# Two attention blocks on one core: the first block's output tiles move into a written-out cycle of one whole unit of the second block

## The chip, the core and the metric

The kernel runs on one core of a Trainium2 chip. The metric is device time in microseconds (us) of one execution; the number compared is the median of several executions. Five engines take part: TensorE (PE, with its weight loads shown apart as PEld), VectorE (DVE), ScalarE (ACT), GpSimd (POOL), and SyncE (SP), which issues the DMAs. Each runs its own instructions strictly in the order in which the program lists them for it, and waits on semaphores for the others.

## The reference

Both inputs are 2048 tokens wide 512, with 32 heads of 16. Block A is attention with a sliding window of 256 keys, block B is full attention. The result is the two outputs side by side.

```
qkv = (x @ wqkv) -> q, k, v per head           # both blocks
s   = (q @ k^T) * 16 ** -0.5                   # A: only keys j with 0 <= i - j < 256
p   = softmax(s)
out = concat_heads(p @ v) @ wo                 # 2048 x 512, for A and for B
```

## The kernel before

**Tiling.** A unit is one group of four heads (g, 8 of them) times one chunk of 512 queries (c, 4 of them), so that each block has 32 units. Block A is done first, and its order doesn't change here. In the stage of block B a unit has 16 steps, one for each 128 keys. A step is four scores and one weighing.

**What PE does in that stage.** There are four kinds of work, and the strings below name them by letters:

- `s`: one score, one matmul of 51 rows by 512 queries (`scores`, line 713). ACT then takes the exponential out of PSUM (line 720).
- `m`: half of one maximum, one matmul of 48 rows by 512 keys (`max2`, line 557), for a unit that comes one or two units later. DVE reduces it out of PSUM (line 560). Two `m` make a pair; `M` is a pair whose two banks one DVE instruction reduces together. A unit has 64 scores and 64 halves of maxima.
- a digit: that many quarters of a weighing (`weigh2`, line 745), p times v, for 128 queries each. A `4` is a whole weighing: eight instructions in four column tiles of the array, into the one bank 0.
- `g`: one step of two output tiles of block A (`half_step`, line 440), a matmul of 64 rows for each of the two tiles. Two tiles of 128 tokens make a pair of output tiles and take 24 `g`, 12 and then 12 with the row halves exchanged between the two banks. Block A has 16 such tiles, so 8 pairs. ACT copies the two finished banks out (`put_out`, line 868), and SP stores them.

`s`, `m` and `g` use half of the array's rows each, and two that follow each other in different halves run side by side. In the text such an instruction is called a half matmul, and two side by side a slot. A weighing uses the array in another arrangement, so that going from half matmuls to a weighing and back costs time.

**Order.** It is written out by hand: the main loop walks strings of letters, the cycles, and issues what each letter says. Cycles are chosen one after the other:

```
MANY = "ssm4mssMs2msms2sM"
FEW = "msmms4msssmsm4ss"
OUTS = "mgggmmggmsgggmsgmmgmggmm44smgsmmgggsgsmggmssggmggg"
...
        if np_ == total:
            cycle = LAST
        elif two and two[-1][0] <= ns / HG * STEP and max(operands(x[3]) for x in two) <= M.t["PE"]:
            cycle = OUTS
        ...
        else:
            cycle = FEW if lead >= LEADM + 1 / 32 else MANY
```

`ns` counts scores, `np_` pairs of maxima, and `two` are the next two output tiles of block A, taken when they are due and their inputs (`x_o`, the normalised and split heads) are there. Each of `MANY`, `FEW` and `OUTS` has 8 scores, that is 2 of a unit's 16 steps. `MANY` has 4 pairs of maxima, `FEW` has 3, and `OUTS` has 8 with all 24 `g` of a pair of output tiles. An `OUTS` runs ahead with the maxima (`lead`), and `FEW` then gives that lead back. Before the last stage there are 14 MANY, then 8 OUTS and 32 FEW in mixed order, then 192 MANY; then come 11 LAST, which have no maxima.

**Banks.** PSUM has eight banks: 0 for the weighing, and seven that the loop's model of the engines (`Loop`) deals out, to whichever of the allowed ones is free first. `ROOMS` gives the allowed ones for scores and for maxima: in FEW four and three, in MANY three, two for single halves and a fixed two for `M`; in OUTS five in common, since banks 6 and 7 take the two output tiles.

**What hangs on a unit's maxima.** When the last pair of a unit is done, POOL puts together the maxima of four key chunks and splits them into parts (`max_chunk` and `max_finish`, lines 631 to 656). PE then transposes the parts (`max_rows`, line 677), ACT copies them (line 679), and two DMAs write them into rows of the unit's queries. The unit's first score needs these rows. Beside this, POOL normalises finished heads (`normalise_now`, lines 840 to 843).

Of the kernel before, what the change touches and what calls it, by code (L numbers as in the profile page):

```python
# [20 lines left out]
HG = 4  # L21
# [16 lines left out]
STEP = 2.45  # L38
# [2 lines left out]

MANY = "ssm4mssMs2msms2sM"
FEW = "msmms4msssmsm4ss"
OUTS = "mgggmmggmsgggmsgmmgmggmm44smgsmmgggsgsmggmssggmggg"
LAST = "4ssssfssss4"
PACES = {FEW: 2.25, MANY: 2.45, OUTS: 5.4, LAST: 2.45}
ROOMS = {FEW: (range(4), range(4, 7)), MANY: (range(3), range(5, 7)), OUTS: (range(5), range(5)),
         LAST: (range(5), range(5))}
LEADM = 1.25
QU = 2.4  # L50


# [103 lines left out]
class Loop:  # L156
# [51 lines left out]
        self.free[n] = self.act + 100  # L208
        return n

    def halves(self, ready):
        for a in range(2):
            end = self.matmul(a, ready)
        return end

# [19 lines left out]
def attention_kernel(ctx: ExitStack, tc: tile.TileContext, xT, wqk, wv, wo, out):  # L235
# [9 lines left out]
    M = Model()  # L245
    ready = {}
    obank = [None]
    ns = 0
# [65 lines left out]
    ps_all = psum.tile([128, 8, QC], F32, name="ps_all")  # L314
# [114 lines left out]
            half_step(q, pairs, [view(bank) for bank in banks])  # L429
        M.pe("h", CHUNK * 233)  # L430

    def half_step(q, pairs, ps):

        turn, q = divmod(q, 12)
        k, i = divmod(q, 3)
        u, v = ((0, 0), (0, 1), (1, 0))[i]
        for a in range(2):
            l, r = pairs[a ^ turn][k]
            rows = slice(64 * a, 64 * a + 64)
            op = nc.tensor.matmul(ps[a ^ turn], l(u)[rows], r(v)[rows], start=turn == q == 0,  # L440
                                  stop=turn == 1 and q == 11)
            if turn and q == a == 0:
                tc.add_manual_dep(op.ins, min(since)[2].ins.name, LANDED, reason="the row tiles change banks")

    def heads_of(b, g, s, a):
# [222 lines left out]
    def max_rows(b, g, c):  # L668
        n = f"{b}_{g}_{c}"
        nm = parts["nm"].bitcast(BF16).rearrange("p a s (n u) -> p a (s n) u", u=2)[:, :, :, 1]  # L670
        if slot[0]:
            bank, ps = None, ps_all[:, 1 + loop.rows()]
        else:
            bank, ps = room()
        ps = ps.bitcast(BF16)
        for a in range(2):
            nc.tensor.transpose(ps[32 * a:32 * a + 32, :128], nm[:, a], ident)  # L677
        nt = sb.tile([64, 128], F32, name=f"ntr_{n}", tag="ntr")
        op = nc.scalar.activation(nt, ps[:64, :128], AF.Copy)
        t = mark(op, M.run("ACT", 200, M.pe("c", 80)))  # L680
        release(bank, t)
        for a in range(2):
            ready["q", b, g, c] = M.dma(12, t)
            nc.sync.dma_start(opq[b, g, c][ROW[a] + KS:ROW[a] + KM].bitcast(F32).rearrange(
                "s r (q t) -> s (r q) t", t=128), nt[32 * a + 8:32 * a + 32])
# [180 lines left out]
    def put_out(b, c, qt, ps):  # L866
        ob = row(f"ob_{b}_{c}_{qt}")
        nc.scalar.activation(ob, ps, AF.Copy)  # L868
        t = M.run("ACT", 480, M.t["PE"] + WAKE)
        nc.sync.dma_start(out[c * QC + 128 * qt:c * QC + 128 * qt + 128, b * D:(b + 1) * D], ob)  # L870
        M.dma(256, t)
        return t

    def pairs_out(b, c, qt):
        return [(lambda u, p=p: osp[b, p, c][:, u, 128 * qt:128 * qt + 128], lambda v, p=p: ws[b, "o", p][:, v])
                for p in range(NG // 2)]
# [89 lines left out]
    def operands(it, n=0):  # L966

        f, b, *a = it
        if f == project_qk:
            keys = [("w", b, a[0], a[1])] + [("x", b, a[2], i) for i in range(4)]  # L970
            t = (slots_st + [M.NEVER] * 2)[n] - 2700 + LAND_V
        elif f == project_v:
            keys = [("w", b, "v", i) for i in range(4)] + [("x", b, a[0], i) for i in range(4)]
            t = (slots_v + [M.NEVER] * 2)[n] - 2700 + LAND_V
        else:
            keys = [("w", b, "o", i) for i in range(4)] + [("o", b, i, a[0]) for i in range(4 if len(a[1]) == 1 else 3)]
            t = 0
        return max(t, *(ready.get(k, M.NEVER) for k in keys))
# [137 lines left out]
    stage, two, banks, turned = 0, None, None, None  # L1116
    todo_a = list(ORDER_A)
    while todo_a or gen[0]:
# [7 lines left out]
        x = "p" if gen[0] else todo_a[0]  # L1126
# [5 lines left out]
        t = NEVER  # L1132
        if gen[0]:
            t = pe
# [118 lines left out]
    loop = Loop()  # L1253
# [9 lines left out]
    while nq < 4 * len(steps):  # L1263
        two = heapq.nsmallest(2, proj)
        lead = np_ / 32 - ns / 64
        if np_ == total:
            cycle = LAST
        elif two and two[-1][0] <= ns / HG * STEP and max(operands(x[3]) for x in two) <= M.t["PE"]:
            cycle = OUTS
            two = [heapq.heappop(proj)[3][1:] for _ in two]  # L1270
            two = [(b, c, qts[0]) for b, c, qts in two]
            nh, ready_h, end_h = 0, max(loop.free[5:]) + loop.SEM, 0
            now[0] = ns / HG * STEP
        else:
            cycle = FEW if lead >= LEADM + 1 / 32 else MANY
        loop.rooms = ROOMS[cycle]
        for x in cycle:
            k = ns // HG
            if x == "s" and k < len(steps):
                if ns % HG == 0:  # L1280
                    t = k * STEP
                    t0 += int(1000 * PACES[cycle])
                    M.t["PE"] = max(M.t["PE"], t0)
                    settle()
                    while todo and todo[0][0] <= t:
                        pop()
                scores(1, *steps[k], ns % HG)
                side = ns % 2
                ns += 1
            elif x in "Mm" and np_ < total:  # L1290
                if not filled:
                    filled = True
                    for _ in range(FILL):
                        nc.tensor.matmul(ps_all[:, 0, 0:256], mone[:, 0], mone, start=True, stop=True)
                if x == "M":
                    sides = (0, 1)
                elif other is None:
                    sides = (0,) if cycle == MANY else (1 - side,)
                    other = 1 - sides[0]
                else:  # L1300
                    sides, other = (other,), None
                u, n = divmod(np_, 32)
                kc, n = divmod(n, 8)
                g, c = units[NA + u][1:]
                n1 = loop.maximum(sides)
                max2(g, c, kc, *divmod(n, 2), sides, ps_all[:, 1 + n1:1 + n1 + len(sides)])
                side = sides[-1]
                if other is None:
                    np_ += 1
                    if np_ % 8 == 0 and np_ % 32 > 8:  # L1310
                        max_chunk(g, c, np_ % 32 // 8 - 1)
                    if np_ % 32 == 0:
                        max_finish(1, g, c)
                        rows.append((k + 1, (1, g, c)))
            elif x == "g":
                if nh == 12:
                    ready_h = max(ready_h, loop.first + loop.SEM)
                half_step(nh, [pairs_out(*y) for y in two], [ps_all[:, 6], ps_all[:, 7]])
                end_h = loop.halves(ready_h)
                nh += 1  # L1320
                if nh == 12:
                    since.clear()
                    loop.first = M.NEVER
                if nh == 24:
                    for n1, y in enumerate(two):
                        put_out(*y, ps_all[:, 6 + n1])
                        loop.copies(5 + n1, end_h)
            elif x == "f" and k < len(steps) and not rows:

                for _ in range(6):  # L1330
                    if gen[0] or proj and proj[0][0] <= k * STEP and operands(proj[0][3]) <= M.t["PE"]:
                        advance()
                        loop.outs(0, 1)
                        half_tile += 1
                        if half_tile % 12 == 0:
                            advance()
                t0 += 650
            elif x.isdigit():
                if 0 <= nq < 4 * len(steps):
                    g, c, kt = steps[nq // 4]  # L1340
                    q = nq % 4
                    weigh2(g, c, kt, 128 * q, 128 * (q + int(x)))
                    loop.weigh(int(x))
                    if kt == NT - 1 and q + int(x) == 4:
                        unit_end(1, g, c)
                nq += int(x)

                if rows and rows[0][0] <= k and nq % 8 == 0:
                    max_rows(*rows.pop(0)[1])
    assert not rows  # L1350
    normalise(1, NG // 2 - 1, NQC - 1)
    while todo or proj or gen[0] or soon:
# [28 lines left out]
```

## Time and profile before

| | us |
|---|---|
| median of 3 runs | 1805.34 (1803.41 to 1806.23) |
| profiled execution | 1804.34 |
| its span, first to last instruction | 1802.6 |

The granted TensorE clock was 0.997 over the span. Stages of block B in the profiled execution, by the start of the first exponential of each:

| stage | from, us | to, us | scores |
|---|---|---|---|
| 14 MANY | 519.0 | 587.5 | 112 |
| 8 OUTS and 32 FEW | 587.5 | 821.1 | 320 |
| 192 MANY | 821.1 | 1716.6 | 1536 |
| 11 LAST | 1716.6 | 1764.7 (last exponential) | 80 |

A row of the timeline gives start, duration, engine, line, operation, what it writes and reads, the number of instructions merged into it, and in brackets the engine's idle time before it with what ended it. A matmul shown with x8 is eight instructions. Durations of single matmuls are longer than the distance between them, since they overlap: starts are what counts.

### The profile page before, as it was taken

The page shows a single profiled execution, that of the slowest core. Times are in us where ns is not written, and L with a number is a line of the kernel's source. Part 1 is how long each engine was busy: PE and PEld are TensorE (multiplying, and loading weights), DVE is VectorE, ACT ScalarE, POOL GpSimd, SP SyncE. Part 2 cuts the span into 40 slices and gives each one's busy share as a digit, 9 for nine tenths or more (in the row PEclk, how much of TensorE's full clock was granted, in tenths as well). Part 3 has the DMA queues.
Part 4 walks back from the last instruction along what each step waited for, and adds up shares of the span by engine and source line. Part 5 has one row for each costly group of instructions (what it writes and reads, how often), then busy time and mean ns, then how long its engine had stood idle before and what let it go on. Part 6 is the DMA issues. An engine that isn't in the chain of part 4 may idle for free.

```text
span 1802.6 us, 39006 instructions
## 1 busy us (share of the span) xinstructions
PE 1779.8 (99%) x14926; PEld 913.2 (51%) x14926; DVE 1524.2 (85%) x2324; ACT 1403.5 (78%) x2749; POOL 648.6 (36%) x1334
## 2 busy tenths in 40 slices
PE   8999999999999999999999999999999999999998
PEld 6776657767754555433444444444444444444436
DVE  4766786677789888889999999999999999999901
ACT  4466676655569676799999998999999999999983
POOL 0377888655745331034311024231012322022320
PEclk9999999999999999999999999999999999999999
DMA  8776667545562122311200311130031121010112
GB/s 266 200 215 192 192 205 226 172 144 173 188 195 81 66 98 61 77 29 48 60 23 31 66 39 29 31 77 16 16 77 35 29 64 37 17 54 8 32 37 94
DMA packets 129355, 166.80 MB, mean 93 GB/s; under 512 B 23204, under 2 KB 59044, under 8 KB 129156
## 3 DMA queue, kind: packets, MB, share of 16 engines
q1 hardware_dynamic: 129168, 164.31, 31.3%
q8 instruction: 117, 1.92, 0.5%
q14 instruction: 70, 0.57, 0.1%
HBM read 94.49 MB, written 68.19 MB: 90 GB/s over the span
## 4 chain that ended last, share of the span: by engine, by line
PE 90%; DVE 5%; ACT 2%; DMA 2%; SPq 1%; issue 1%; POOL 0%; ACTq 0%; DVEq 0%; POOLq 0%
PE ps_all L745 28%; PE ps_all L557 19%; PE ps_all L713 18%; PE ps_all L440 10%; PE ps_all L305 8%; PE ps_all L760 4%; DVE mt L560 4%; PE ps_all L603 3%; ACT p L720 1%; DMA in<-xT_A 1%; DVE nm L613 1%; SPq L469 0%; PE ps_all L677 0%; DVE ps_all L612 0%; ACT ob L868 0%
## 5 line engine op out<-in xcount | busy, mean ns | idle before, releaser
L720 ACT ACTIVATE p<-ps_all 128x512 f32<-128x512 f32 x2432 | 1263.5, 598 | 214.1 <-PE ps_all L713 129.2
L560 DVE TENSOR_REDUCE mt<-ps_all 128x1 f32<-128x512 f32 (+1 forms) x1596 | 1209.5, 832 | 52.8 <-PE ps_all L557 42.6
L713 PE MATMUL ps_all<-oq,opk 51*128 51x512 f32 (+2 forms) x2752 | 757.6, 406 | 4.0 <-ACT p L720 1.5
L557 PE MATMUL ps_all<-opk,oq 48*128 48x512 f32 x2016 | 672.5, 436 | 2.0 <-ACT ob L868 0.9
L745 PE MATMUL ps_all<-p,vt 128*17 128x256 f32 (+1 forms) x5736 | 576.7, 476 | 1.8 <-ACT ou L771 1.7
L713 PEld LDWEIGHTS ps_all<-oq,opk 51*128 51x128 f32 x2752 | 389.1, 186 | 194.9 <-ACT p L720 156.1
L557 PEld LDWEIGHTS ps_all<-opk,oq 48*128 48x128 f32 x2016 | 311.9, 185 | 305.8 <-DVE mt L560 187.1
L731 POOL TENSOR_SCALAR_AFFINE_SELECT p<-p 128x256 f32<-128x256 f32 x480 | 179.0, 407 | 113.0 <-ACT p L720 111.8
L745 PEld LDWEIGHTS ps_all<-p,vt 128*17 128x17 f32 x5736 | 97.2, 95 | 223.5 <-issue 210.8
L612 DVE COPY_PREDICATED ps_all<-mone,ps_all 128x256 f32<-128x256 uint16 x224 | 95.4, 426 | 84.7 <-PE ps_all L603 78.6
L613 DVE TENSOR_REDUCE nm<-ps_all 128x2 f32<-128x512 f32 x224 | 155.3, 693 | 7.7
L629 POOL TENSOR_TENSOR mu<-mt 128x16 f32<-128x16 f32 x31 | 6.9, 222 | 405.2 <-DVE mt L560 405.2
L631 POOL TENSOR_TENSOR mu<-mt,mm 128x16 f32<-128x16 f32 x62 | 13.7, 220 | 385.4 <-DVE mt L560 385.4
L440 PE MATMUL ps_all<-x,w 64*128 64x512 f32 x720 | 119.2, 393 | 0.0
L305 PE MATMUL ps_all<-x,w 128*128 128x512 f32 x408 | 102.7, 400 | 2.0 <-ACT x L253 1.3
L760 PE MATMUL ps_all<-p,vt 128*17 128x384 f32 (+2 forms) x1408 | 95.4, 391 | 0.0
L603 PE MATMUL ps_all<-opk,oq 48*128 48x384 f32 (+2 forms) x512 | 92.3, 364 | 2.4 <-ACT vst L504 0.8
L799 POOL TENSOR_TENSOR rd<-ld,minus 128x32 f32<-128x32 f32 x15 | 81.9, 5458 | 20.2 <-DMA ld<-od 20.2
L440 PEld LDWEIGHTS ps_all<-x,w 64*128 64x128 f32 x720 | 84.5, 185 | 8.8
L305 PEld LDWEIGHTS ps_all<-x,w 128*128 128x128 f32 x408 | 74.2, 188 | 24.3 <-ACT p L720 2.7
L388 ACT ACTIVATE raw<-ps_all 128x512 f32<-128x512 f32 x56 | 32.3, 596 | 67.9 <-PE ps_all L305 53.1
L440 PE MATMUL ps_all<-w_v,x 64*128 64x512 f32 x432 | 81.1, 391 | 0.0
(79 smaller groups left out, 1039.6 us busy)
## 6 DMA issues: line engine op xcount, KB each, us to landing
parts<-st SPq DMA_DIRECT2D x64, 512.0 KB
oq<-parts SPq DMA_DIRECT2D x128, 128.0 KB
opk<-parts SPq DMA_DIRECT2D x128, 128.0 KB
od<-ou SPq DMA_DIRECT2D x64, 256.0 KB
vd<-vst SPq DMA_DIRECT2D x32, 272.0 KB
oq<-parts SPq DMA_DIRECT2D x128, 64.0 KB
opk<-parts SPq DMA_DIRECT2D x128, 64.0 KB
t<-od SPq DMA_DIRECT2D x32, 256.0 KB
```

Of the source, the lines that this page charges most:

```text
L305: nc.tensor.matmul(ps, l(u), r(v), start=start and k == 0, stop=stop and k == n - 1)
L440: op = nc.tensor.matmul(ps[a ^ turn], l(u)[rows], r(v)[rows], start=turn == q == 0, stop=turn == 1 and q == 11)
L557: nc.tensor.matmul(ps[:, a - lo], q[rows, 128 * qt:128 * qt + 128], k[rows, kc * QC:kc * QC + QC], start=True, stop=True)
L560: op = nc.vector.tensor_reduce(out=m[:, kc, lo:lo + len(sides), r, qt], in_=ps, axis=AX.X, op=ALU.max)
L603: nc.tensor.matmul(two[:, a, 0:w], opq[b, g, c][rows, r, 128 * qt:128 * qt + 128], opk2(g)[rows, r, t0:t1], start=True, stop=True)
L612: nc.vector.copy_predicated(two[:, :, 256:384], later, two[:, :, 0:128])
L613: op = nc.vector.tensor_reduce(out=m[:, :, r, qt, 0], in_=two[:, :, 128:384], axis=AX.X, op=ALU.max)
L713: nc.tensor.matmul(ps[x][:, col:col + n1], opk2(g)[rows, pr, 128 * k:128 * k + 128], opq[b, g, c][rows, pr, q0:q0 + n1], start=True, stop= ...
L720: op = nc.scalar.activation(p[:, a0 + x, :w], ps[x][:, :w], AF.Exp, scale=SCALE)
L731: nc.gpsimd.affine_select(out=v, in_=v, pattern=[[0, 2], [sign, 128]], compare_op=ALU.is_ge, fill=zero_fill, base=base, channel_multiplier ...
L745: nc.tensor.matmul(o[32 * j:32 * j + VW, q0:q1], vt[(g // 2) % 2][:, kt, vc:vc + VW], pts[1, g, c, kt, j // 2][:, j % 2, q0:q1], start=kt ...
L760: nc.tensor.matmul(o[32 * j:32 * j + VW, q0:q0 + w], vt[(g // 2) % 2][:, kt, vc:vc + VW], pts[b, g, c, m, j // 2][:, j % 2, col:col + w], ...
```

## The change

OUTS becomes a cycle of a whole unit: 64 scores, 32 pairs of maxima, all as single halves `m`, 16 weighings and the 24 `g` of one pair of output tiles. It begins only where the scores stand at 56 of a unit's 64 (`PHASE`), so that it runs from eight scores before one unit's end to eight before the next one's. Four new letters change the allowed banks on the way: `[` allows all seven for scores and maxima in common, `(` five in common (banks 6 and 7 go to the output tiles from here on), `)` issues the two copies of the finished tiles and allows seven again, and `]` goes back to four and three. The letter `t` gives the place of the transposes inside the cycle; in the other cycles they stand where they did. A `g` now starts with the row half that the instruction before it did not use.

With that there are 15 MANY, 8 OUTS of a unit each, one after the other, then 167 MANY, and the same 11 LAST; FEW is not used any more. The work in the stage is the same: the 8 units hold the 512 scores and 256 pairs of maxima that 24 MANY, 32 FEW and 8 OUTS held.

```
-OUTS = "mgggmmggmsgggmsgmmgmggmm44smgsmmgggsgsmggmssggmggg"
+OUTS = "[smssmm4ssmsmms4smsssmm4mmssmms4smmmss4smmmss4msmmss(4smmgsgsgmgsmsggmsggmsgmsmggmgmmm44msgmsggsmsgmsggmsgmgsmgsmggmsgmm)4mssmss4smsmsm4smsmms4msssmm4smmsmss4smsmtssmmmss4s]"
-PACES = {FEW: 2.25, MANY: 2.45, OUTS: 5.4, LAST: 2.45}
+PACES = {FEW: 2.25, MANY: 2.45, OUTS: 2.6, LAST: 2.45}
-ROOMS = {FEW: (range(4), range(4, 7)), MANY: (range(3), range(5, 7)), OUTS: (range(5), range(5)),
-         LAST: (range(5), range(5))}
+ROOMS = {FEW: (range(4), range(4, 7)), MANY: (range(3), range(5, 7)), OUTS: (range(4), range(4, 7)),
+         LAST: (range(5), range(5)), "[": (range(7), range(7)), "(": (range(5), range(5)),
+         ")": (range(7), range(7)), "]": (range(4), range(4, 7))}
+PHASE = 56
...
-    def half_step(q, pairs, ps):
+    def half_step(q, pairs, ps, first=0):
-        for a in range(2):
+        for a in (first, 1 - first):
...
-            if turn and q == a == 0:
+            if turn and q == 0 and a == first:
                 tc.add_manual_dep(op.ins, min(since)[2].ins.name, LANDED, reason="the row tiles change banks")
...
-        elif two and two[-1][0] <= ns / HG * STEP and max(operands(x[3]) for x in two) <= M.t["PE"]:
+        elif two and ns % 64 == PHASE and two[-1][0] <= ns / HG * STEP and max(operands(x[3]) for x in two) <= M.t["PE"]:
             cycle = OUTS
-            nh, ready_h, end_h = 0, max(loop.free[5:]) + loop.SEM, 0
...
+            elif x in "[()]":
+                loop.rooms = ROOMS[x]
+                if x == "(":
+                    nh, ready_h, end_h = 0, max(loop.free[5:]) + loop.SEM, 0
+                if x == ")":
+                    for n1, y in enumerate(two):
+                        put_out(*y, ps_all[:, 6 + n1])
+                        loop.copies(5 + n1, end_h)
             elif x == "g":
-                half_step(nh, [pairs_out(*y) for y in two], [ps_all[:, 6], ps_all[:, 7]])
-                end_h = loop.halves(ready_h)
+                half_step(nh, [pairs_out(*y) for y in two], [ps_all[:, 6], ps_all[:, 7]], 1 - side)
+                end_h = loop.halves(ready_h, 1 - side)
...
-                if nh == 24:
-                    for n1, y in enumerate(two):
-                        put_out(*y, ps_all[:, 6 + n1])
-                        loop.copies(5 + n1, end_h)
...
-                if rows and rows[0][0] <= k and nq % 8 == 0:
+                if rows and rows[0][0] <= k and nq % 8 == 0 and cycle != OUTS:
                     max_rows(*rows.pop(0)[1])
+            elif x == "t" and rows:
+                max_rows(*rows.pop(0)[1])
```

Three places show it. The line numbers after the change are two higher (557 becomes 559, 713 becomes 715, 745 becomes 747, 440 becomes 442). In the rows `opk` and `oq` are keys and queries, with the operand named first telling scores (`oq` first) from maxima (`opk` first); `w_o` and `x_o` are the weights and inputs of an output tile, `p` and `vt` those of a weighing.

PE, the last steps of a pair of output tiles of block A's second 512 tokens before the change, up to the weighing behind them:

```order
L440 MATMUL ps_all<-w_o_6686,x_o_2_1_7790 128x512 x4
L557 MATMUL ps_all<-opk_76,oq_1_0_7869 128x512
L440 MATMUL ps_all<-w_o_6777,x_o_3_1_7993 128x512 x6
L557 MATMUL ps_all<-opk_76,oq_1_0_7869 128x512
L713 MATMUL ps_all<-oq_0_2_6760,opk_75 128x512
L557 MATMUL ps_all<-opk_76,oq_1_0_7869 128x512 x2
L713 MATMUL ps_all<-oq_0_2_6760,opk_75 128x512
L745 MATMUL ps_all<-p_0_2_8_0_8319,vt_77 17x512 x2
L745 MATMUL ps_all<-p_0_2_8_1_8370,vt_77 17x512 x2
```

The same on PE after the change:

```order
L442 MATMUL ps_all<-w_o_6686,x_o_2_1_7790 128x512 x2
L715 MATMUL ps_all<-oq_1_0_7850,opk_76 128x512
L559 MATMUL ps_all<-opk_76,oq_1_1_8342 128x512
L442 MATMUL ps_all<-w_o_6777,x_o_3_1_7955 128x512 x4
L559 MATMUL ps_all<-opk_76,oq_1_1_8342 128x512
L715 MATMUL ps_all<-oq_1_0_7850,opk_76 128x512
L442 MATMUL ps_all<-w_o_6777,x_o_3_1_7955 128x512 x2
L559 MATMUL ps_all<-opk_76,oq_1_1_8342 128x512 x2
L747 MATMUL ps_all<-p_1_0_5_0_9068,vt_77 17x512 x2
L747 MATMUL ps_all<-p_1_0_5_1_9083,vt_77 17x512 x2
```

Runs of up to six `g` matmuls with one half of a maximum between them become runs of two to four with a score or a maximum on either side, and the cycle's weighings go on behind them without a change of cycle.

ACT, the two copies `ob` of finished output tiles among the exponentials, before:

```order
L720 ACTIVATE p_0_1_13_0_7937<-ps_all 128x512 x2
L720 ACTIVATE p_0_1_13_1_7952<-ps_all 128x512 x2
L868 ACTIVATE ob_0_0_7968<-ps_all 128x512
L868 ACTIVATE ob_0_1_7971<-ps_all 128x512
L720 ACTIVATE p_0_1_14_0_7997<-ps_all 128x512 x2
L679 ACTIVATE ntr_0_2_8037<-ps_all 64x128
```

And after:

```order
L722 ACTIVATE p_0_2_7_0_8193<-ps_all 128x512 x2
L722 ACTIVATE p_0_2_7_1_8214<-ps_all 128x512 x2
L870 ACTIVATE ob_0_0_8232<-ps_all 128x512
L870 ACTIVATE ob_0_1_8235<-ps_all 128x512
L722 ACTIVATE p_0_2_8_0_8245<-ps_all 128x512 x2
L722 ACTIVATE p_0_2_8_1_8252<-ps_all 128x512 x2
```

The copies of the first pair stand behind key tile 13 of unit (0, 1) before, and behind key tile 7 of unit (0, 2) now; their two stores move with them on SP's queue.

PE, a unit's transposes (`ident`, `nm`) before the change, the first of two alike, where a weighing stands right ahead of them and a pair of output tiles right behind:

```order
L557 MATMUL ps_all<-opk_76,oq_1_0_7869 128x512
L745 MATMUL ps_all<-p_0_2_9_0_8389,vt_77 17x512 x2
L745 MATMUL ps_all<-p_0_2_9_1_8404,vt_77 17x512 x2
L677 LDWEIGHTS nm_73
L677 MATMUL ps_all<-ident,nm_73 32x128
L713 MATMUL ps_all<-oq_0_2_6760,opk_75 128x512 x2
L557 MATMUL ps_all<-opk_76,oq_1_0_7869 128x512
L440 MATMUL ps_all<-w_o_6439,x_o_0_1_7676 128x512 x6
```

And after:

```order
L747 MATMUL ps_all<-p_1_0_10_1_9249,vt_77 17x512 x2
L715 MATMUL ps_all<-oq_1_0_7850,opk_76 128x512
L559 MATMUL ps_all<-opk_76,oq_1_2_8825 128x512
L715 MATMUL ps_all<-oq_1_0_7850,opk_76 128x512
L559 MATMUL ps_all<-opk_76,oq_1_2_8825 128x512
L679 LDWEIGHTS nm_73
L679 MATMUL ps_all<-ident,nm_73 32x128
L715 MATMUL ps_all<-oq_1_0_7850,opk_76 128x512 x2
L559 MATMUL ps_all<-opk_76,oq_1_2_8825 128x512 x3
L715 MATMUL ps_all<-oq_1_0_7850,opk_76 128x512 x2
L747 MATMUL ps_all<-p_1_0_11_0_9254,vt_77 17x512 x2
```

The transposes now stand in the middle of a run of 11 half matmuls, 13 scores ahead of the next unit's first score.

More of the change, by code (lines that the diff above doesn't have):

```diff
@@ L209, in rows, with halves @@
         return n
-    def halves(self, ready):
-        for a in range(2):
+    def halves(self, ready, first):
+        for a in (first, 1 - first):
             end = self.matmul(a, ready)
@@ L436, in half_step @@
         u, v = ((0, 0), (0, 1), (1, 0))[i]
-        for a in range(2):
+        for a in (first, 1 - first):
             l, r = pairs[a ^ turn][k]
```

## Prediction

> **What bounds the kernel now.** I read the page's totals first, then cut the span into windows at the first exponentials of the stages, then listed the waits of the stage that the change rewrites, and last its timeline on PE.
>
> ```profile
> span 1802.6 us, 39006 instructions
> PE 1779.8 (99%) x14926; PEld 913.2 (51%) x14926; DVE 1524.2 (85%) x2324; ACT 1403.5 (78%) x2749; POOL 648.6 (36%) x1334
> ```
>
> PE is busy nearly all the time, but overlapped matmuls count as busy, so what a stage costs must come from its length. The windows (us, then busy time and instructions of each engine), and the count of exponentials in the first:
>
> ```profile
> core 0: us, PE busy (x) PEld busy (x) DVE busy (x) ACT busy (x) POOL busy (x), PEclk, DMA share, GB/s
> 587.49:937.97 350.48, 345.72 (x2673) 161.38 (x2673) 316.56 (x469) 284.94 (x553) 97.50 (x197) 1.00 0.21 59
> 782.70:816.80 34.10, 34.10 (x244) 13.10 (x240) 30.14 (x49) 33.30 (x66) 11.73 (x18) 1.00 0.15 37
> 937.97:1716.59 778.62, 778.48 (x6729) 316.05 (x6728) 778.61 (x1003) 704.55 (x1378) 176.27 (x424) 1.00 0.15 38
> 587.49:937.97 350.48, 272.79 (x520) 1.00 0.21 59
> ```
>
> The third window is MANY alone, 1336 scores, which is 167 cycles of 4.66 us; DVE is busy in all of it, so DVE sets MANY. The second is eight FEW of 4.26 us; PE is busy in all of it and DVE in 88%, so PE sets FEW. The first holds 520 scores: one MANY that stays, and the 24 MANY, 32 FEW and 8 OUTS that eight new units replace. These take 350.48 - 4.66 = 345.8 us, or 43.2 us for each unit of 64 scores. Taking out 24 x 4.66 = 111.8 and 32 x 4.26 = 136.3 leaves 97.7 us for eight OUTS, 12.2 us each, with what they do to the cycles behind them.
>
> **What PE's work costs, from one FEW.** PE's timeline, three weighings with the half matmuls between them:
>
> ```profile
> 786.59 1.05 PE L745 MATMUL ps_all<-p,vt 128*17 128x512 f32 x8
> 787.58 0.50 PE L557 MATMUL ps_all<-opk,oq 48*128 48x512 f32 x1
> 787.58 0.73 PE L713 MATMUL ps_all<-oq,opk 51*128 51x512 f32 x3
> 788.15 0.51 PE L557 MATMUL ps_all<-opk,oq 48*128 48x512 f32 x2
> 788.39 0.40 PE L713 MATMUL ps_all<-oq,opk 51*128 51x512 f32 x1
> 788.71 1.05 PE L745 MATMUL ps_all<-p,vt 128*17 128x512 f32 x8
> ...
> 790.51 0.40 PE L557 MATMUL ps_all<-opk,oq 48*128 48x512 f32 x1
> ...
> 308.09 1.54 PE L440 MATMUL ps_all<-w_v,x 64*128 64x512 f32 x12
> 649.65 1.91 PE L745 MATMUL ps_all<-p,vt 128*17 128x512 f32 x16
> 651.49 0.49 PE L713 MATMUL ps_all<-oq,opk 51*128 51x512 f32 x1
> ```
>
> Twelve half matmuls in six slots take 1.54 us and the last lasts 0.40, so a slot is (1.54 - 0.40) / 5 = 0.23 us. A weighing and the way back from it take 787.58 - 786.59 = 0.99 us, and a second one right behind adds 651.49 - 649.65 - 0.99 = 0.85. From the first half matmul to the next weighing are 1.13 us for seven halves, four slots: 0.92, and 0.21 for the way there.
>
> **The new unit on PE.** It has 64 + 64 + 48 = 176 half matmuls, 88 slots if all go in twos. Its 16 weighings stand in 15 places (two are adjacent in the middle of the output steps), with 15 runs between them, six of which are odd (7 or 11), which costs half a slot each: 91 slots. That is 91 x 0.23 = 20.9, 15 x (0.99 + 0.21) = 18.0, and 0.85: 39.8 us.
>
> The transposes come on top, now in the middle of a run. Their place of before shows little, so I bound them:
>
> ```profile
> 602.99 1.91 PE L745 MATMUL ps_all<-p,vt 128*17 128x512 f32 x16
> 604.71 0.22 PE L677 MATMUL ps_all<-ident,nm 128*32 128x128 bf16 x2
> 604.87 0.49 PE L713 MATMUL ps_all<-oq,opk 51*128 51x512 f32 x1
> PEld L677 <- POOL nm L656: 12.1, 27, 1.2
> ```
>
> Behind two weighings they add 604.87 - 602.99 - 1.84 = 0.04 us. Inside a run PE must leave the halves and come back, which I bound by 0.21 + 0.16 (604.71 to 604.87) and the 0.14 by which the way back from a weighing exceeds the 0.85, 0.5 in all. I take 0.5, since the place resembles the way to a weighing more than the old place. Then PE waits for POOL's parts: 12.1 / 27 = 0.45 us a time now, and I take that again. So a unit is 39.8 + 0.5 + 0.45 = 40.75 us.
>
> **DVE and ACT beside it.** Rows of single reductions (the first merges three) and what POOL does with the last of a unit:
>
> ```profile
> 656.60 1.89 DVE L560 TENSOR_REDUCE mt<-ps_all 128x1 f32<-128x512 f32 x3 [0.58 <-PE ps_all L713]
> 596.94 0.69 DVE L560 TENSOR_REDUCE mt<-ps_all 128x1 f32<-128x512 f32 x1 [0.17 <-PE ps_all L557]
> 586.66 0.22 POOL L631 TENSOR_TENSOR mu<-mt,mm 128x16 f32<-128x16 f32 x1 [4.86 <-DVE mt L560]
> 588.75 0.22 POOL L656 TENSOR_TENSOR nm<-nr,nm 128x16 bf16<-128x16 f32 x1
> 588.93 1.29 POOL L840 TENSOR_TENSOR t<-t,bl 128x512 f32<-128x512 f32 x1
> 590.97 1.27 POOL L843 TENSOR_TENSOR x_o<-t,x_o 128x512 fp32r<-128x512 f32 x1
> ```
>
> A reduction comes every (1.89 - 0.69) / 2 = 0.60 us, so 64 singles are 38.4 us: DVE is 94% full and no bound over the unit, but close. That 48 doubles turn into 96 singles costs nothing as long as this cover of 2.3 us a unit holds. ACT's 64 exponentials and two copies are 284.94 / 520 x 64 = 35.1 us of busy time, copies and others in it, also under 40.75.
>
> MANY leaves DVE full, so the first unit starts with DVE behind. I price this at one waiting double reduction, at most 1.2 us (two singles), and take 1.1.
>
> **The sum.** Eight units: 8 x 40.75 = 326.0, and 1.1: 327.1 us instead of 345.8, 18.7 less. The profiled execution took 1804.34 us, 1.00 under the median of 1805.34; 1804.34 - 18.7 = 1785.6, and by the median 1786.6. I say 1787.
>
> Where the gain comes from can be followed in the other direction. An OUTS of 12.2 us has 72 half matmuls and two adjacent weighings, and its last halves join the next cycle's run: 36 x 0.23 + 0.99 + 0.85 + 0.21 = 10.3, so 1.9 us of it are waits, 15 us over eight. They are these:
>
> ```profile
> PEld ps_all L557 <- DVE mt L560: 28.1, 36, 0.9
> ACT p L720 <- PE ps_all L557: 27.3, 17, 3.4
> DVE mt L560 <- PE ps_all L557: 22.1, 44, 1.3
> PEld ps_all L557 <- ACT ob L868: 4.5, 10, 0.9
> POOL t L840 <- DMA bl<-rl: 18.4, 3, 11.5
> ```
>
> They belong to 587.5 to 821 us. ACT and DVE stand idle while PE runs output steps, and then PE waits for reductions and for the copies `ob` that free two of the banks of the next maxima. In the new unit the output steps are spread over 17 scores and 23 maxima, and all seven banks are open to both kinds afterwards. The rest is fewer changes of arrangement: 24 x 3 + 32 x 2 + 8 = 144 before, 8 x 15 = 120 now.
>
> **What moves at no cost.** Sixteen stores `out<-ob` go to SP later; nothing on PE reads them, and their buffers are shared with transfers that are as dense now. Block A's `x_o` tiles live longer; block B takes their buffers over in the same order, the first of them after the output steps that read it. The wait at the change of row halves now goes to a reduction two weighings (1.84 us) old; that costs nothing while DVE is less than that behind.
>
> **Rivals.**
>
> *DVE and the banks take half back.* Between `(` and `)` stand 23 reductions, 13.8 us of DVE, over 44 slots and the two adjacent weighings with a change before and after, 10.1 + 0.99 + 0.85 + 0.21 = 12.2 us of PE, in five banks. DVE falls 1.6 us behind there. If all of it stops PE, a unit is 42.35 and the time 1786.6 + 8 x 1.6 = 1799. For it: MANY, where DVE is the bound. Against it: the five banks can hold two waiting maxima (1.2 us), and DVE has 2.3 us of slack elsewhere in the unit. The Trainium skill's "TensorEngine Tiling (Array Packing)", section Performance Considerations, says that packing the array speeds up TensorE but not the emptying of PSUM, which may then become the bottleneck. MANY agrees with it (DVE 778.61 of 778.62 us); by that rule alone a unit would still last only its 38.4 us of reductions.
>
> *The old waits return.* If, on top of that 1.6 us, the copies hold the banks as before (4.5 us over eight, 0.56 each), a unit loses 2.2 us: 1786.6 + 8 x 2.2 = 1804, no change. For it: in both kernels banks 6 and 7 come free only when ACT has copied the tiles. Against it: behind `)` any free bank will do, where FEW had three fixed ones for its maxima, two of them these.
>
> *Slower: POOL's queue stops PE at the transposes.* PE can't pass the `t`. Between the last maximum's matmul and `t` PE has two weighings and 6.5 slots, 2 x 1.20 + 6.5 x 0.23 = 3.9 us; the reduction (0.69) and POOL's chain (586.66 to 588.97, 2.3) need 3.0 of them. A normalisation ahead of the chain adds 3.3 us (588.93 to 592.24), and its first instruction waited 18.4 / 3 = 6.1 us for its DMA when it waited at all: 9.4 - 0.9 = 8.5 us for one such hit. Two make it 1804, no change; it decides from three, with which the time is 1786.6 + 25.5 = 1812. Against it: the longest wait of this kind is 1.2 us now, and in the order of POOL's queue no normalisation stands between the last two chains of any of the eight units; one reciprocal does, in the seventh.
>
> *The change doesn't take place.* The order shows eight units, each with its 24 output steps, so this is out.
>
> **Chances.** As forecast, 1781 to 1792: 0.70. DVE and banks, 1792 to 1800: 0.14. Better, with no wait at all (8 x 39.8 = 318.4, 1778 to 1781): 0.05. Old waits return: 0.06. Slower by POOL: 0.05. The range 1780 to 1799 leaves less than 2 in 10 out. A difference of 0.2%, 3.6 us, is about what a measurement of this kernel can tell from none; faster by more than that are the first three cases, 0.89, within it 0.06, slower 0.05.
>
> **What the profile after would show.** The stretch from the first new unit to the eighth's end should be about 327 us long for 512 exponentials. PE's waits for `ob` should be gone and ACT's waits for PE's maxima down to a few us. DVE should be busy in some 94% of the stretch; if it is busy all through, the first rival holds. The wait of the transposes for POOL should stay under 0.5 us each; some of several us would be the slower rival. MANY must still take 4.66 us a cycle. The prediction is wrong if a slot costs more than 0.23 us where output steps, scores and maxima alternate one by one, which no row of before shows over a long run.

## The result and the profile after

The changed kernel takes 1782.9 us in the median of four executions (1782.06 to 1783.07), against 1804.38 us (1801.71 to 1806.23): a ratio of 0.9881, with a 95% interval of 0.9864 to 0.9898. The profiled execution took 1782.06 us, its span 1780.3. The forecast was 1787.

The page after, and its windows: one MANY, the eight new units together with it, the first four units, the eighth, and all MANY behind them.

```profile
span 1780.3 us, 38761 instructions
PE 1761.9 (99%) x14734; PEld 908.2 (51%) x14734; DVE 1525.8 (86%) x2372; ACT 1403.0 (79%) x2749; POOL 650.7 (37%) x1334
```

```profile
core 0: us, PE busy (x) PEld busy (x) DVE busy (x) ACT busy (x) POOL busy (x), PEclk, DMA share, GB/s
583.34:588.13 4.79, 4.79 (x44) 2.15 (x43) 4.79 (x8) 4.28 (x10) 3.02 (x9) 1.00 0.00 0
583.34:916.88 333.54, 331.91 (x2495) 160.11 (x2498) 321.13 (x521) 284.56 (x554) 98.37 (x199) 1.00 0.22 62
588.13:630.47 42.34, 42.12 (x310) 20.37 (x309) 40.66 (x66) 35.14 (x69) 18.38 (x32) 1.00 0.25 80
630.47:671.59 41.12, 40.91 (x308) 19.69 (x306) 39.44 (x65) 34.93 (x69) 16.49 (x29) 1.00 0.24 81
671.59:712.43 40.84, 40.62 (x307) 19.66 (x306) 39.34 (x65) 35.07 (x69) 3.89 (x17) 1.00 0.44 97
712.43:753.24 40.81, 40.59 (x308) 19.66 (x306) 39.36 (x65) 35.02 (x69) 13.16 (x24) 1.00 0.15 44
876.00:916.88 40.88, 40.68 (x308) 19.36 (x311) 39.35 (x65) 35.01 (x69) 7.06 (x20) 1.00 0.10 31
916.88:1695.28 778.40, 778.40 (x6728) 315.60 (x6720) 777.71 (x1002) 704.89 (x1378) 176.95 (x424) 1.00 0.15 38
```

The stage that took 350.48 us takes 333.54, so 16.9 us less. The 1336 scores of MANY behind it take 778.4 us, where they took 778.6. The span shrank by 22.3 us. Some 2 of the other 5 belong to the change as well: the old first OUTS began ahead of the boundary of that window, with output steps before its first score (its first six `g` matmuls start at 584.99, its first exponential at 587.50). Up to the last exponential ahead of that boundary the 14 MANY run alike in both kernels to 0.03 us, and at the boundary the old one is 2.05 us behind.

```profile
584.99 1.47 PE L440 MATMUL ps_all<-w_o,x_o 64*128 64x512 f32 x6
587.50 0.60 ACT L720 ACTIVATE p<-ps_all 128x512 f32<-128x512 f32 x1 [1.96 <-PE ps_all L557]
```

The remaining 3 us lie in block A (2.1) and behind the last exponential (0.9). Nothing was changed there, and block B's first exponential, at 519.0 us before, starts anywhere from 514.7 to 520.0 us in the profiled executions told of below. So I put 19 us of the gain down to the stage, and compare from here on the time of the eight units in the traces: 328.75 us after the change (333.54 - 4.79). Each experiment below is one execution. How well a stretch repeats can be seen on the 167 MANY behind the units, the same program in every kernel: 778.2 to 778.6 us in all of them.

The waits in the eight units, which answer to those of before:

```profile
PEld ps_all L715 <- DVE mt L562: 34.5, 42, 0.9
PEld ps_all L715 <- ACT p L722: 34.0, 40, 0.9
PEld ps_all L559 <- DVE mt L562: 27.2, 32, 0.9
ACT p L722 <- PE ps_all L559: 10.0, 26, 2.9
DVE mt L562 <- PE ps_all L559: 7.8, 29, 0.4
PEld L679 <- POOL nm L658: 5.2, 8, 0.7
POOL t L842 <- DMA bl<-rl: 14.2, 3, 5.8
```

The copies `ob` no longer appear in them. DVE's waits for maxima on PE fell from 22.1 to 7.8 us, though the stretch is longer. The first three rows are mostly the 0.85 us between a weighing's weight loads and the next ones; such rows aren't PE idle, and they stay as long in the run below in which ACT and DVE are both relieved.

### The profile page after: what moved, and what is told of

Its sections match the earlier page's. It is cut to its first block, busy times and chain, and to the rows that moved or that the text cites. A ratio compares the mean times of both kernels' runs of the same rounds, so it can differ in the third digit from the quotient of the medians.

```text
span 1780.3 us, 38761 instructions
## 1 busy us (share of the span) xinstructions
PE 1761.9 (99%) x14734; PEld 908.2 (51%) x14734; DVE 1525.8 (86%) x2372; ACT 1403.0 (79%) x2749; POOL 650.7 (37%) x1334
## 4 chain that ended last, share of the span: by engine, by line
PE 90%; DVE 4%; DMA 2%; ACT 1%; SPq 1%; issue 1%; POOL 1%; POOLq 0%; ACTq 0%; DVEq 0%
PE ps_all L747 28%; PE ps_all L559 19%; PE ps_all L715 18%; PE ps_all L442 10%; PE ps_all L307 8%; PE ps_all L762 4%; PE ps_all L605 3%; DVE mt L562 2%; ACT p L722 1%; DMA in<-xT_A 1%; DMA parts<-st 1%; SPq L471 0%; PE ps_all L679 0%; DMA in<-xT_B 0%; DVE nm L615 0%
## 5 line engine op out<-in xcount | busy, mean ns | idle before, releaser
L559 PE MATMUL ps_all<-opk,oq 48*128 48x512 f32 x2016 | 661.8, 436 | 0.2
L715 PEld LDWEIGHTS ps_all<-oq,opk 51*128 51x128 f32 x2752 | 381.7, 185 | 219.0 <-ACT p L722 149.1
L559 PEld LDWEIGHTS ps_all<-opk,oq 48*128 48x128 f32 x2016 | 303.9, 184 | 277.2 <-DVE mt L562 167.7
```

The costliest lines, as they stand in the source:

```text
L559: nc.tensor.matmul(ps[:, a - lo], q[rows, 128 * qt:128 * qt + 128], k[rows, kc * QC:kc * QC + QC], start=True, stop=True)
L715: nc.tensor.matmul(ps[x][:, col:col + n1], opk2(g)[rows, pr, 128 * k:128 * k + 128], opq[b, g, c][rows, pr, q0:q0 + n1], start=True, stop= ...
```

## Experiments

Each kernel is one edit of the changed kernel, unless it says otherwise, and shows the time of the eight units beside 328.75.

**Half reductions.** In `max2`, inside the eight units half of the keys are left out of each maximum:

```
-        op = nc.vector.tensor_reduce(..., in_=ps, axis=AX.X, op=ALU.max)
+        op = nc.vector.tensor_reduce(..., in_=ps[:, :, 0:QC // 2] if slot[0] and loop.outs_now else ps, ...)
```

> The changed kernel, but inside the eight new units each reduction reads only 256 of its 512 columns (half of each maximum is left out), so DVE's work in a unit falls from 39.35 us of busy time to some 22; order and banks stay. Theory (PE sets the unit, 39.8 us of its own and 0.5 for the transposes): units go from 40.85 to 40.3 to 40.8 us, the first from 42.34 to about 41, the eight together 2 to 6 us shorter. Rival (DVE, 96% busy, and the banks it holds set the unit): the eight are 8 us or more shorter.

Its third and fourth units:

```profile
675.44:716.29 40.85, 40.85 (x307) 19.82 (x306) 24.30 (x65) 35.02 (x69) 3.86 (x17) 1.00 0.44 97
716.29:757.12 40.83, 40.83 (x307) 19.82 (x306) 24.31 (x65) 34.96 (x69) 13.13 (x24) 1.00 0.16 44
```

DVE fell from 39.35 to 24.3 us and the unit stayed at 40.85. The eight took 328.16, 0.6 less, and nearly all of that in the first unit (41.83). DVE, 96% busy, does not set the unit alone. Even the theory expected more.

**Half exponentials, and both.** In `scores` (inside the eight units the exponentials of half of the queries are left out, and the weighing reads the written half twice; it takes 1.05 us as before):

```
-            op = nc.scalar.activation(p[:, a0 + x, :w], ps[x][:, :w], AF.Exp, scale=SCALE)
+            we = QC // 2 if b and (loop.outs_now or (g, c, kt) in halved) else w
+            op = nc.scalar.activation(p[:, a0 + x, :we], ps[x][:, :we], AF.Exp, scale=SCALE)
```

> The changed kernel, but inside the eight units each exponential covers only 256 of its 512 queries (the weighing then reads these 256 twice, same size on PE), so ACT's exponentials take some 0.2 us less each; DVE, order and banks stay. Moving the transposes changed nothing: PE, freed of them, waited in the run of halves instead. Theory A (that wait is for ACT's exponentials): units fall by 0.4 us or more, 3 us or more over eight. Theory B (it is for DVE's reductions, or PE's own): under 1.5 us.

> Half exponentials and half reductions together in the eight units, so that neither ACT nor DVE can hold a bank that PE wants for long: what is left is PE's own work, the copies and POOL. By the sum of the prediction a unit is then 39.8 us and what the transposes cost, 0.04 to 0.5: 39.8 to 40.3, 4 to 8 us less over eight than the changed kernel. Rival (PE's own work is dearer than the sum says): a unit stays within 0.3 us of 40.85.

The fourth unit of each, half exponentials first:

```profile
710.00:750.69 40.69, 40.49 (x308) 18.44 (x306) 39.27 (x65) 23.05 (x69) 13.11 (x24) 1.00 0.16 44
708.62:748.83 40.21, 40.21 (x308) 18.90 (x306) 24.29 (x65) 22.85 (x69) 13.13 (x24) 1.00 0.16 45
```

Half exponentials alone: 326.92, 1.8 us less, which is between what the two theories said; a unit falls by 0.15. With both, the unit takes 40.21 us, in the 39.8 to 40.3 that the sum gave, and the eight 322.25, 6.5 us less. That PE is shown busy in all of it proves nothing, since it is in the 40.85 us with half reductions too. But the waits for ACT and DVE that are left are, to some 0.2 us in all, the 0.85 us behind each weighing:

```profile
PEld ps_all L717 <- DVE mt L563: 34.2, 41, 0.9
PEld ps_all L717 <- ACT p L727: 34.0, 40, 0.9
PEld ps_all L560 <- DVE mt L563: 27.2, 32, 0.9
```

So 40.2 us is PE's own work, and some 0.65 us a unit are waits. Half exponentials alone take away 0.15 of them, half reductions none, and both together all.

PE's rows say where they are. The run of halves that holds the transposes takes, from the weighing ahead of it to the one behind it, 3.32 us in the changed kernel's second unit (666.27 to 669.59), and 2.94 with both relieved (663.70 to 666.64). In the changed kernel PE waits there for POOL's parts (the row of L679 above, 5.2 us in eight waits). With half exponentials it still does (5.1 us in eight), and the run takes 3.33 us (664.16 to 667.49). With half reductions POOL has its last maximum earlier (1.9 us in five waits) and the wait moves: the transposes start in time, but the maxima behind them wait for exponentials, and the run takes 3.32 us again (670.13 to 673.45). Two waits of nearly the same size lie side by side there, and one alone can't be won. The other 0.26 us are in the two long runs between `(` and `)`: 6.45 and 7.33 us in the mean of the third to seventh units, 6.33 and 7.19 with both relieved.

**The banks taken back, in both parts and in one.**

```
-         LAST: ..., "[": (range(7), range(7)), "(": (range(5), range(5)),
-         ")": (range(7), range(7)), "]": ...
+         LAST: ..., "[": (range(4), range(4, 7)), "(": (range(5), range(5)),
+         ")": (range(4), range(4, 7)), "]": ...
```

> The changed kernel with the seven common banks taken back: at [ and behind ) scores have four banks and maxima three, as in the old FEW; five in common between ( and ). Theory (the order, which spreads the output steps, brings most of the gain; banks matter only where the copies hold two of them): 0.6 to 1.1 us a unit, the eight 4.5 to 9 us longer. Rival (the common banks bring it): 15 us or more, the whole gain is gone.

> The changed kernel with the seven common banks only in the first part of the cycle, from [ to (; behind ) four for scores and three for maxima as in the old FEW. With the old banks in both parts the eight units were 17.8 us longer. Theory A (fixed banks make PE wait wherever scores and maxima alternate unevenly, so each part pays for itself; the last part has 43 of the 88 halves outside the parentheses): about 8 to 10 us longer than the changed kernel. Theory B (it is the two banks held by the copies, so only the part behind ) matters): 14 us or more longer.

> The changed kernel with the seven common banks only behind ); from [ to ( four for scores and three for maxima. Theory A (each part pays for itself): about 8 to 10 us longer than the changed kernel over the eight units. Theory B (only the part behind ) matters): 4 us or less.

The fourth unit with the old banks in both parts, with common banks in the first part only, and in the last part only:

```profile
719.91:763.05 43.14, 42.77 (x307) 20.27 (x306) 39.90 (x65) 35.49 (x69) 13.12 (x24) 1.00 0.14 42
720.90:762.31 41.41, 41.35 (x307) 19.96 (x306) 39.40 (x65) 35.04 (x69) 13.14 (x24) 1.00 0.16 43
717.05:759.28 42.23, 41.72 (x308) 20.18 (x306) 39.84 (x65) 35.41 (x69) 13.15 (x24) 1.00 0.15 42
```

The eight took 346.60 us with the old banks (17.9 more), 333.09 with the old banks only behind `)` (4.3 more) and 339.44 with them only ahead of `(` (10.7 more). Without common banks nearly the whole gain of the stage is gone: 351.37 us with its MANY, against 350.48 before the change, or 352.5 with the 2.05 us that lie ahead of that window. Of the theory and the rival of the first run, the rival holds. Of the two theories on the parts neither holds: the parts don't pay alike, and it isn't the two banks of the copies, since the part ahead of `(` costs more than twice the other.

The same run of halves in the third unit shows how it works. PE's timeline with common banks (the changed kernel), and then with the old ones:

```profile
675.96 1.05 PE L747 MATMUL ps_all<-p,vt 128*17 128x512 f32 x8
676.94 0.50 PE L559 MATMUL ps_all<-opk,oq 48*128 48x512 f32 x2
677.28 0.40 PE L715 MATMUL ps_all<-oq,opk 51*128 51x512 f32 x2
677.51 0.39 PE L559 MATMUL ps_all<-opk,oq 48*128 48x512 f32 x2
677.75 0.40 PE L715 MATMUL ps_all<-oq,opk 51*128 51x512 f32 x1
678.08 1.05 PE L747 MATMUL ps_all<-p,vt 128*17 128x512 f32 x8
```

```profile
681.16 1.05 PE L747 MATMUL ps_all<-p,vt 128*17 128x512 f32 x8
682.14 0.51 PE L559 MATMUL ps_all<-opk,oq 48*128 48x512 f32 x2
682.48 0.40 PE L715 MATMUL ps_all<-oq,opk 51*128 51x512 f32 x2
682.72 0.39 PE L559 MATMUL ps_all<-opk,oq 48*128 48x512 f32 x1
683.42 0.50 PE L559 MATMUL ps_all<-opk,oq 48*128 48x512 f32 x1 [0.32 <-DVE mt L562]
683.43 0.50 PE L715 MATMUL ps_all<-oq,opk 51*128 51x512 f32 x1
683.86 1.05 PE L747 MATMUL ps_all<-p,vt 128*17 128x512 f32 x8
```

The run has four maxima. With three banks for them the fourth has to wait for a reduction, PE stands, and from weighing to weighing it takes 2.70 us instead of 2.12. It is the only run of four ahead of `(`, and by the same measure, in the mean of the third to seventh units, it accounts for 0.57 of the 2.3 us that a unit loses. The rest is spread: 0.4 us in the first run behind `)`, 0.1 to 0.2 in most others. Most of these hold no more than three maxima, and why each waits was not followed further.

**Common banks in the old order.** The kernel before, with one entry changed:

```
-ROOMS = {FEW: (range(4), range(4, 7)), ...
+ROOMS = {FEW: (range(7), range(7)), ...
```

> The kernel before, with seven common banks for scores and maxima in FEW, nothing else. Theory (the waits for the copies are 4.5 us, the rest of the old cycle's 15 us of waits comes from output steps in a lump): the stretch of OUTS and FEW, 233.6 us, becomes 4 to 6 us shorter. Rival (the banks bring the gain): 10 us or more shorter. A third way: no change, since in FEW PE is the bound anyway.

The stretch of OUTS and FEW took 230.9 us, 2.7 less than the 233.6 of before. That is less than the theory said and far from the rival's 10. So neither half of the change does it alone: the new order without the common banks brings some 1 us, common banks in the old FEW 2.7, both together 19. MANY and OUTS kept their banks in this run; common banks in all of the old order were not run, and neither was the new entry of `PACES` by itself.

**The output steps in lumps.** Inside the parentheses:

```
-(4smmgsgsgmgsmsggmsggmsgmsmggmgmmm44msgmsggsmsgmsggmsgmgsmgsmggmsgmm)
+(4smmsgggmsmgggsmsmgggsmsmgggsmmmm44msmsgggmsmgggsmsmgggsmsmgggsmsmm)
```

> The changed kernel with the 24 output steps between the parentheses written in runs of three, as in the old cycle, instead of one and two at a time; the letters in each stretch between weighings are the same, only their order differs, and banks, sides and transposes stay. Theory (in a lump PE feeds neither ACT nor DVE, and then has to wait for them: the old cycle's 1.9 us of waits a pair of output tiles): 1 to 1.9 us a unit, 8 to 15 us over the eight, all of it between ( and ). Rival (five banks of queue cover three steps, 0.7 us, and the common banks alone made the gain): under 3 us.

The fourth unit took 41.91 us, the eight 336.59, 7.8 more. The mean time from a unit's 24th to its 41st exponential (third to eighth unit), which is the part between the parentheses, went from 13.81 to 14.95 us; the parts on either side moved by less than 0.1. That is the lower end of what the theory said, and not the rival's: with the common banks, spreading the steps is worth about 1 us a pair of output tiles.

**More changes of arrangement.** Four of a unit's weighings cut in two, everywhere two halves apart, for example:

```
-smmmss4smmmss4msmmss(
+smmmss2sm2mmss2ms2mmss(
```

> The changed kernel with four of a unit's sixteen weighings cut in two, two or three half matmuls apart, the same work in four more changes of the array's arrangement (and, where a run becomes odd, half a slot). Theory (a change there and back costs 0.21 + 0.14 = 0.35 us and nothing covers it): 4 x 0.35 = 1.4 us a unit, with one to two half slots 1.5 to 1.6, 11 to 13 us over eight. Rival (the changes hide in waits for DVE and ACT): under 4 us. It bears on the 24 changes that the new order saves, 8 us by this price.

The fourth unit took 42.15 us, the eight 338.26, 9.5 more: 0.30 us for each of 32 changes (0.33 in a steady unit), with no odd run added. They are paid in full, though a little below the 0.35 of the forecast.

**The row half on which a step starts.**

```
-half_step(nh, ..., [ps_all[:, 6], ps_all[:, 7]], 1 - side)
-end_h = loop.halves(ready_h, 1 - side)
+half_step(nh, ..., [ps_all[:, 6], ps_all[:, 7]], 0)
+end_h = loop.halves(ready_h, 0)
```

> The changed kernel with every output step starting on the first half of the rows, as before the change, instead of on the half that the instruction ahead did not use. Of the cycle's 18 runs of output steps 8 then start on the half that was just used. Theory (PE sets the unit and a pair that doesn't fit costs half a slot, 0.115 us, at the run's start and its end): 8 x 0.23 = 1.8 us a unit at most, 7 to 15 us over eight. Rival (PE has slack, the order of halves doesn't matter): under 2 us.

The eight took 329.97 us, 1.2 more: the rival's case. This part of the change is worth little.

**The transposes behind the last weighing.**

```
-smsmtssmmmss4s]
+smsmssmmmss4ts]
```

> The changed kernel with the transposes moved from the middle of the run of 11 halves to right behind the unit's last weighing, 5 scores later. Theory (they cost 0.5 us in a run and 0.04 behind a weighing, and PE then no longer waits for POOL there, 0.45): a unit 0.5 to 0.9 us shorter, 4 to 7 us over eight. Rival (the change of arrangement there is needed anyway for the scores and maxima that follow, and the later place costs as much): within 2 us, or longer if the next unit's first score then waits for its rows.

The eight took 328.92 us, 0.2 more: the rival's case. At the end of the second unit, PE ran the 11 halves without the transposes and then the weighing with them behind it:

```profile
664.95 1.05 PE L747 MATMUL ps_all<-p,vt 128*17 128x512 f32 x8
665.94 0.49 PE L715 MATMUL ps_all<-oq,opk 51*128 51x512 f32 x1
...
666.75 0.99 PE L559 MATMUL ps_all<-opk,oq 48*128 48x512 f32 x3
667.61 0.73 PE L715 MATMUL ps_all<-oq,opk 51*128 51x512 f32 x2
668.26 1.05 PE L747 MATMUL ps_all<-p,vt 128*17 128x512 f32 x8
669.13 0.23 PE L679 MATMUL ps_all<-ident,nm 128*32 128x128 bf16 x2
669.29 0.49 PE L715 MATMUL ps_all<-oq,opk 51*128 51x512 f32 x2
```

Behind the weighing they add next to nothing (669.29 - 668.26 = 1.03), as the row of before said. But the run of six slots takes 2.32 us (665.94 to 668.26) instead of 6 x 0.23 + 0.21 = 1.59: the wait at the transposes had given ACT time to free banks, and without it PE waits for ACT there (its weight loads stand still for exponentials for 0.41 and 0.18 us). With the weighing ahead, this run takes 3.31 us without the transposes and 3.32 with them. This kernel's total, 1780.81 us in one execution, is no evidence of a gain; its eight units are not shorter.

**No output steps.** All `g` taken out of the cycle, so that these output tiles aren't computed.

> The changed kernel without the 24 output steps in each of the eight units (block A's output projection is left out; the two copies and stores of each pair stay). Theory: PE loses 24 slots of 0.23 us, 5.5 us, and is then no longer the bound; DVE with 39.35 us is, so a unit takes about 39.4 instead of 40.85 and the eight are about 12 us shorter. If PE alone set the time they would be 44 us shorter. Rival (DVE and banks set the unit already): 3 us shorter or less, the output steps cost next to nothing.

The eight took 353.54 us, 24.8 longer than with the steps, which neither theory allowed. The reason is the clock. Its second unit, three-microsecond pieces of it, and the two adjacent weighings in the last of them:

```profile
635.11:681.03 45.92, 45.52 (x259) 17.27 (x258) 39.38 (x65) 35.10 (x69) 16.40 (x29) 0.85 0.21 73
645.00:648.00 3.00, 3.00 (x26) 0.80 (x24) 3.00 (x6) 2.66 (x6) 1.75 (x2) 1.00 0.45 134
648.00:651.00 3.00, 3.00 (x16) 1.64 (x12) 3.00 (x6) 2.73 (x6) 0.69 (x3) 1.00 0.52 199
651.00:654.00 3.00, 2.98 (x10) 1.46 (x9) 3.00 (x6) 2.02 (x4) 2.70 (x5) 0.61 0.05 19
654.00:657.00 3.00, 3.00 (x17) 0.49 (x16) 2.03 (x4) 0.00 (x0) 2.85 (x4) 0.50 0.00 0
654.16 3.61 PE L747 MATMUL ps_all<-p,vt 128*17 128x512 f32 x16
```

Between the parentheses DVE, with 23 reductions, now sets the pace, PE issues a half matmul only when a bank comes free, and the granted clock falls to half; then the two weighings take 3.6 us instead of 1.9. What the steps cost at full clock the run can only hint at: the fourth unit took 42.20 us at a mean clock of 0.96 and the second 45.92 at 0.85, and a straight line through the two gives about 41 us at full clock, an estimate, and no less than the 40.85 with the steps. What it does show is that leaving the steps out of this order makes it longer: with them PE is dense enough to keep its clock.

## Why the prediction was right, step by step

**The unit's price** was 40.75 us and is 40.85 (40.81 to 41.02 from the third unit on). With ACT and DVE relieved, PE's own work is 40.2 us: that term held. By the prediction's prices the transposes' run is 0.99 + 6 x 0.23 + 0.21 = 2.58 us without them and it took 2.94 in that kernel, so they cost 0.36, not 0.5. POOL's term, 0.45, is the 0.38 us that this run loses in the changed kernel (3.32 against 2.94), but POOL is not its only cause: with POOL out of the way the run waits as long for ACT. That is why moving the transposes brought nothing. The 0.26 us of waits between `(` and `)` were priced at nothing. So the unit came out within 0.1 us partly by luck: some 0.2 us too much in two terms stands against some 0.3 left out.

**The entry into the first unit** was priced at 1.1 us; the first unit took 1.5 more than a steady one and the second 0.3. With half reductions the first took 1.0 more, and with both halves 0.6, so DVE's arrears from MANY are part of it and ACT's another; the cause of the 0.6 stays open.

**The sum**, 327.1 us for the eight, was 328.75, so 1.65 too low. What the eight replace was too low as well: its 345.8 us start at the first exponential of the first OUTS, and 2.05 us of that OUTS lie ahead of it. That the 18.7 us of the forecast meet the 19 of the stage is these two misses, which nearly cancel. The measured median lies 4 us below the forecast, and some 3 of them are in parts of the span that the change doesn't touch.

**Where the gain comes from** is the step that was wrong in its weights. I put 15 us down to output steps in lumps, the rest to 24 fewer changes of arrangement, and the common banks only beside them. (At the 0.35 us that its rows give for one, these changes alone would be 8.4 us; 15 and 8.4 are more than its sum of 18.7.) By the runs the changes are worth 24 x 0.30 = 7 us and spreading the steps 8, but both were measured with the seven common banks in place, and without these the new order is within some 1 us of the old. The three prices overlap and can't be added up. The old banks cost 2.2 us a unit in the mean, which is the number of the prediction's second rival, but by chance: the rival made it up of 1.6 us between `(` and `)` and 0.56 for the copies. With the old banks only behind `)`, where the copies are, 4.3 of the 17.9 us are lost; with them only ahead of `(` 10.7, and the largest single piece of it is the run with more maxima than three banks hold.

**The rivals.** DVE as the bound was out: half of its work away moved nothing in a steady unit. POOL never stopped PE for long: 5.2 us in eight waits, the longest 0.7. That is 0.65 a time, though, more than the 0.5 that the prediction gave as a sign, and ACT's waits for PE's maxima, 10.0 us, are more than a few. In its list of signs the one for DVE (some 94% busy; it was 96%) could not have told a bound from a nearly full engine, and only the run with less DVE work did.

## What to carry to other kernels

Where an in-order engine feeds two others through a few buffers, look at the longest run of requests to one of them, not only at their sum: a fixed share of three banks stalled PE on a run of four maxima though DVE had time to spare over the unit, and a common pool removed it. An order and a pool had to be changed together here, since each alone was worth 1 to 3 us and both 19. And a short wait that one removes may be the one in which others catch up: a run with the suspected engine's work halved tells more than its share of busy time. Where two waits end at nearly the same time, halve both: here one alone brought 0.6 or 1.8 us, and both 6.5.

## What the runs showed of the hardware

The granted clock of TensorE fell to 0.50 without an idle gap in the profile. In the kernel without output steps it fell inside the piece from 651 to 654 us, where its mean is 0.61. In the 3 us ahead, 648 to 651, the profile shows PE busy in 3.00 of 3.00 us, but with 16 matmuls, where the piece before had 26; the changed kernel has 44 in 5 us (650 to 655), and the clock stays full. A matmul's end is modelled in the profile, so short gaps in the array itself may not show. Thin work was enough here; how thin it has to be, no run measured.

The Trainium skill's "TensorE: Matmul & The Clock Gate", in its Part 1, says that a monitor of PE's recent activity halves the clock, and its section "Why this matters for your kernels" advises to avoid idle gaps of more than some 3 us between bursts. The half clock agrees; a gap of that length does not stand in the profile here.

A half matmul that starts on the row half just used costs far less than a slot lost: eight such starts a unit cost 0.2 us in all, where the slot count says up to 1.8. The 0.26 us of waits in that part of the unit can hide a little of such a cost, but not 1.8.
